# Attention with banded heads, then expert routing: masks by quadrants, a swapped half of v, routing steps and one weight load moved

## The chip, the cores and the metric

The kernel runs on one core of a Trainium2 chip. The metric is the device time of one execution in microseconds. Engines are named as in the profile: PE (matrix), DVE (vector), ACT (scalar), POOL (GpSimd) and SP (sync); PEld is the weight load of PE.

## The reference

```python
def _attn_ref(q, k, v, is_retrieval, n_sink, window):      # q, k, v: 4 x 8 x 768 x 64
    scores = scale * np.matmul(q, k.transpose(0, 1, 3, 2))
    rel = pos[:, None] - pos[None, :]
    causal = rel >= 0
    stream_keep = causal & ((pos[None, :] < n_sink) | ((rel >= 0) & (rel < window)))   # 4 and 64
    # heads with is_retrieval = [1,0,1,0,0,0,1,0] use causal, the others stream_keep
    a = softmax(where(mask, scores, -1e9))
    return np.matmul(a, v)

def _moe_ref(x, domain_id, w1, w2):                         # x: 3072 x 512, 8 experts
    for e in range(E):
        mask = domain_id == e
        out[mask] = np.maximum(x[mask] @ w1[e], 0.0) @ w2[e]   # w1: 512 x 1024, w2: 1024 x 512

x = attn_out.transpose(0, 2, 1, 3).reshape(B * S, H * D)
return _moe_ref(x, moe_domain_id, moe_w1, moe_w2)
```

Three of the eight heads attend to all earlier positions. The five others see a band of 64 positions and the first four positions ("sinks"). Every token then goes through the two layers of the one expert that its `domain_id` names.

## The kernel before

**Attention.** Heads are taken two at a time: `PAIRS = [(0, 2), (6, 7), (1, 3), (4, 5)]` for each of four batches, so 16 pairs, numbered n. The first pair of a batch has two full heads and six rounds, the second one full and one banded head and four rounds, the other two are fully banded with two rounds. Two rounds make a step, so these pairs have three, two, one and one steps. A pair goes through: load q, k (`load_qk`, L140) and v (`load_v`, L160) in float32 by SP's queue; cast to half precision on POOL (`cast_qk`, `cast_v`); twelve transposes on PE into qT and kT, copied out of PSUM by ACT or DVE (L303); masks and scores (`scores`, L306); exponentials on ACT (L341); the products with v (`av_items`, L345, with its matmuls at L384); division by the row sums on DVE (L396, L397). In qT and kT the first head of a pair has rows 0 to 63 and the second head rows 64 to 127.

Masks are added by the matrix engine before the scores: a matmul of the identity with a constant of 0 and -30000 (L313) writes the mask into PSUM, and the score matmuls (L330) add to it. In a banded head, keys are cut into blocks of 64. An even block's scores stand in partitions 0 to 63 and an odd block's in 64 to 127, each for 128 queries.

**Order of the work.** All queues run in the order in which the program writes them. The main loop (L846) takes pair n: `hooks(n)` puts out SP's loads for pair n + 4, POOL's casts for n + 2 and n + 1, the store of a finished batch's x (`store_x`, L409) and for some n the expert weights; then each step has the scores of pair n, followed by the transposes of pair n + 1 or the value products of pair n - 1. For the first pair the program writes the order out (L861). q and k have three float32 buffers each, v has four.

**Routing.** `routing_items` (L415) computes on DVE which token belongs in which slot of which expert. Its parts are put after given steps by a table from (pair, step) to functions (L632). They end with `map_i`, `map_e` (row numbers of x for gathers) and `out_i`.

**Experts.** `load_w(e, which)` (L191) loads one weight of 2 MB in float32 as 1 MB in half precision through POOL's queue. `load_xe(pr, g)` (L652) gathers 128 rows of x for slot group g of a pair of experts, also through POOL's queue. Groups 0, 1, 3, 4 of experts 0 to 3 gather from the first three batches (`map_e`), so they may start before the last batch is stored; the groups 2, 5 and 6 need all of x. PE transposes the rows (`x_transpose`, L665), multiplies with w1 (`layer1`, L694), ACT applies relu (L711), PE multiplies with w2 (L754, L768), DVE copies (L718), and POOL scatters the rows (L720). The order on PE is written out from L878: first 256 columns of experts 0 to 3, then the transposes of groups 2, 6 and 5 and the remaining columns, then the second layers.

Of the kernel before, what the change touches and what calls it, by code (L numbers as in the profile page):

```python
# [21 lines left out]
def kernel(  # L22
# [46 lines left out]
    up = jj >= 64  # L69
    cc = ii[:, :64]  # L70
    m_even = neg(np.where(up, cc < kk, cc >= kk))
    m_odd = neg(np.where(up, cc >= kk, cc < kk))
    m_first = neg((ii[:, :P] >= jj) & ((jj < NS) | (ii[:, :P] - jj < WIN)))
# [6 lines left out]
            m_first,  # L80
            np.tile(np.concatenate([m_even, m_odd], axis=1), (1, 4)),
# [7 lines left out]
    C_ID, C_DG, C_S0, C_S1, C_ST, C_ON, C_IO = (  # L89
        0, 128, 256, 384, 896, 1024, 1026)  # L90
# [68 lines left out]

    def load_v(b, pi):  # L160
        hA, hB = PAIRS[pi]
        t = vpool.tile([P, 2, NSO, D], FP32, tag="v32", name=f"v32_{b}_{pi}")
        for hh, h in enumerate((hA, hB)):
            nc.sync.dma_start(
                out=t[:, hh], in_=v[b, h].rearrange("(c p) d -> p c d", p=P)
            )
        v_t[b, pi] = t
# [57 lines left out]
    def s_bin(col, hh, part):  # L225
        res = []
        q0, q1 = ((0, 512), (512, S))[part]

        def add(k0, m, o, i0, w, kind="band"):
            lo, hi = max(i0, q0), min(i0 + w, q1)  # L230
            if lo < hi:
                res.append((col + lo - q0, hi - lo, hh, k0, m, o, lo, (hh, kind)))

        for o in (0, 64):
            add(o, 64, o, 0, P)
        for it in range(NSO):
            k0 = it * P
            if it:
                add(k0, 64, 0, k0, P)
            add(k0 + 64, 64, 64, k0 + (64 if it else P), P if it else 64)  # L240
        if part == 1:
            for r in range(4):
                i0 = (P, 3 * P, 4 * P, 4 * P)[r]
                res.append((col + 256, 256, hh, 0, 32, 32 * r, i0, (hh, "s", r)))
        return res

    def plan(ra, rb):

        dg = lambda c: (c, P, C_DG)
        s0 = lambda c: (c, 512, C_S0)  # L250
        s1 = lambda c: (c, 256, C_S1)
        if ra and rb:
            return [
                (r_bin(0 if n < 5 else 384, 0, n), r_bin(512, 1, n),
                 [dg(0 if n < 5 else 384), dg(512)], 0 if n < 5 else 384,
                 1024 if n < 5 else 640)
                for n in range(6)
            ]
        if ra:
            return [  # L260
                (r_bin(0, 0, 0, 64), s_bin(512, 1, 0), [dg(0), s0(512)], 0, 1024),
                (r_bin(0, 0, 1, 64), s_bin(512, 1, 1), [(0, P, C_DG), s1(512)], 0, 1024),
                (r_bin(0, 0, 2), r_bin(512, 0, 3), [dg(0), dg(512)], 0, 1024),
                (r_bin(384, 0, 5), r_bin(512, 0, 4), [dg(384), dg(512)], 384, 1024),
            ]
        return [
            (s_bin(0, 0, 0), s_bin(512, 1, 0), [s0(0), s0(512)], 0, 1024),
            (s_bin(0, 0, 1), s_bin(512, 1, 1), [s1(0), s1(512)], 0, 1024),
        ]
# [36 lines left out]
    def scores(n, rounds):  # L306
        sps = {}
        for r in rounds:
# [3 lines left out]
            for c, w, col in plans[n % 4][r][2]:  # L312
                nc.tensor.matmul(  # L313
                    out=sp[:, c : c + w],
                    lhsT=id_sb,
                    rhs=c16[:, col : col + w],
                    start=c // 512 not in begun,
                    stop=True,
                    skip_group_check=True,
                )  # L320
                begun.add(c // 512)
# [23 lines left out]
    def av_items(n):  # L345
# [5 lines left out]
        def make(hh, h):  # L351
# [8 lines left out]
            else:  # L360
                full.append((slice(0, P), band(0), ve[:, 0, h, :], 0, 0, P))
                for it in range(1, NSO):
# [4 lines left out]
                    )  # L367
                for it in range(1, NSO):
                    low.append((slice(0, 64), band(it * P), ve[0:64, it, h, :], it, 0, P))
                    for m0 in (64, 0):  # L370
                        jt = it if m0 else it - 1
                        upp.append(
                            (slice(64, P), band(it * P + m0), ve[64:P, jt, h, :], it, m0, 64)
                        )
# [32 lines left out]
        return (fa + fb, la + lb + ua + ub) if lb else (fa, fb)  # L407
# [7 lines left out]
    def routing_items():  # L415
# [194 lines left out]
        def rows3():  # L610
# [22 lines left out]
            (0, 0): (one_hot,), (0, 1): (ranks, scan, own, place, place2, split),  # L633
            (1, 0): (high,), (2, 0): (high2,), (3, 0): (high3,), (4, 1): lows[0:1],
            (4, 2): lows[1:2], (5, 1): (flags,), (6, 0): lows[2:3], (7, 0): lows[3:4],
            (8, 1): lows[4:5], (8, 2): lows[5:6], (10, 0): (rows,), (11, 0): (rows2,),
            (12, 1): (rows3,),
# [142 lines left out]
    nc.scalar.dma_start(out=c16[:, 0:C_S0], in_=c16_d[:, 0:C_S0])  # L780
    load_qk(0)
    load_v(0, 0)
    nc.sync.dma_start(out=dom64[:], in_=moe_domain_id.rearrange("(p c) -> p c", p=P))
    nc.sync.dma_start(out=c32[:], in_=c32_d)
    load_qk(1)
    nc.sync.dma_start(out=c16[:, C_S0:], in_=c16_d[:, C_S0:])
    load_v(0, 1)
# [15 lines left out]
    def hooks(n):  # L803
# [13 lines left out]
        if n == 6:  # L817
            load_w(0, 1)
        if n == 13:
# [26 lines left out]
    for n in range(NPAIR + 1):  # L846
# [13 lines left out]
        if n == 0:  # L860
            tr, av0, av1 = [lambda: keep_warm(3, 0)], [lambda: keep_warm(3, 1)], tr  # L861
# [7 lines left out]
    store_x(B - 1)  # L869
    for g in (2, 6, 5):  # L870
        load_xe(0, g)
    load_w(0, 2)
# [164 lines left out]
```

The softmax here doesn't subtract the row's maximum and nothing guards it: scores larger than these inputs give would overflow.

## Time and profile before

| what | value |
|---|---|
| time, median of 4 | 217.18 us (215.89 to 218.42) |
| profiled execution | 218.96 us, span 217.2 us |
| busy share PE, PEld | 87%, 57% |
| busy share DVE, ACT, POOL | 43%, 41%, 55% |
| mean granted PE clock | 0.931 |
| POOL's queue (q0) | 26.80 MB, 54.5% of 16 DMA engines |
| SP's queue (q1) | 22.50 MB, 37.7% |

The shares are means over a span of two unlike halves. A row of the page's slices is one fortieth of the span, 5.4 us, and a digit is tenths. In tables by stage each engine has its busy microseconds with the number of instructions, and then come the granted clock, the DMA share (over 1 where several transfers overlap) and GB/s. In a timeline a line is start, length, engine, source line and operation, and in brackets how long the engine was idle before it and what released it. The page's instruction queues, 19 packets with 0.31 MB and 10 with 0.08 MB, are the fetches of the program itself.

### The profile page before, as it was taken

The numbers are of one execution on the slowest core, as the hardware profiler recorded it, in microseconds if no ns is written. First come the engines' busy times: TensorE is split into PE (matmuls) and PEld (weight loads), VectorE is DVE, ScalarE is ACT, GpSimd is POOL, SyncE is SP. The second block draws the span as 40 slices with busy tenths as digits, with TensorE's granted clock in tenths as the row PEclk, the third lists the DMA queues.
The fourth block names the chain that finished last, engine by engine and source line by source line (L and its number), as shares of the span: only waits on it lengthen the run. The fifth ranks groups of instructions, "written<-read, shape, count | busy, mean of one in ns | idle before, by whom it ended". The sixth has DMA issues, their size and how long they took to land. (4 is left out here: it accounts for less than half of the span.)

```text
span 217.2 us, 5394 instructions
## 1 busy us (share of the span) xinstructions
PE 188.4 (87%) x2256; PEld 124.5 (57%) x2256; DVE 93.6 (43%) x200; ACT 89.9 (41%) x115; POOL 118.9 (55%) x154
## 2 busy tenths in 40 slices
PE   7653997999899898788997999999969999999930
PEld 2332774777578575447997885456534555444420
DVE  4566778478886984052112105520144300333320
ACT  2461687567877975302664560025500156000000
POOL 7737678395166457840287844627776510450571
PEclk9995898599999999659999999999999999999995
DMA  6999999999999988999359999999799999981232
GB/s 186 297 276 307 304 266 259 308 331 233 292 297 319 320 254 149 208 237 201 133 114 210 208 256 235 203 280 289 159 197 211 273 216 224 278 259 51 94 143 90
DMA packets 44447, 49.76 MB, mean 229 GB/s; under 512 B 28799, under 2 KB 37376, under 8 KB 44418
## 3 DMA queue, kind: packets, MB, share of 16 engines
q0 software_dynamic: 9472, 26.80, 54.5%
q1 hardware_dynamic: 34802, 22.50, 37.7%
q8 instruction: 19, 0.31, 0.6%
q10 hardware_dynamic: 144, 0.07, 0.2%
q14 instruction: 10, 0.08, 0.1%
HBM read 56.73 MB, written 10.49 MB: 310 GB/s over the span
## 5 line engine op out<-in xcount | busy, mean ns | idle before, releaser
L341 ACT ACTIVATE eT<-sp 128x1024 f16<-128x1024 f32 (+2 forms) x56 | 50.0, 953 | 23.5 <-PE sp L330 18.6
L711 ACT ACTIVATE hT<-h 128x512 f16<-128x512 f32 (+2 forms) x48 | 31.7, 668 | 61.4 <-PE h L704 58.6
L704 PE MATMUL h<-xT,w 128*128 128x256 f16 (+2 forms) x384 | 50.7, 290 | 2.3 <-DVE xT L683 1.1
L720 POOL DMA_INDIRECT out_dram<-oute,out_i x27 | 27.2, 1006 | 39.0 <-DVE oute L718 25.7
L704 PEld LDWEIGHTS <-w 128*128 128x128 f16 x384 | 39.0, 114 | 12.7 <-issue 1.6
L754 PE MATMUL o<-w,hT 128*128 128x512 f16 x184 | 41.9, 379 | 0.0
L718 DVE COPY oute<-o 128x512 f32<-128x512 f32 x23 | 15.9, 692 | 51.3 <-PE o L754 45.5
L754 PEld LDWEIGHTS <-hT 128*128 128x128 f16 x184 | 17.5, 98 | 19.8 <-issue 0.8
L384 PEld LDWEIGHTS <-eT 128*128 128x128 f16 (+2 forms) x672 | 22.5, 106 | 10.8 <-issue 8.2
L330 PE MATMUL sp<-qT,kT 64*64 64x128 f16 (+8 forms) x468 | 21.8, 258 | 7.1 <-DVE kT L303 6.3
L384 PE MATMUL av<-ve,eT 128*128 128x65 f16 (+2 forms) x572 | 23.5, 202 | 4.2 <-DVE kT L303 1.6
L155 POOL CAST q<-q 128x768 f16<-128x768 f32 x15 | 13.0, 865 | 24.8 <-DMA q<-in_q_dram 19.4
L654 POOL DMA_INDIRECT xe<-x_tok,map_i x16 | 16.3, 1020 | 16.3 <-SPq L941 11.8
L689 DVE COPY xT<-xtp 128x1024 f16<-128x1024 f16 (+1 forms) x16 | 8.9, 554 | 25.4 <-PE xtp L676 25.4
L330 PEld LDWEIGHTS <-kT 64*64 64x64 f16 (+2 forms) x468 | 10.6, 105 | 15.2 <-DVE kT L303 6.7
L397 DVE TENSOR_TENSOR xb<-av,rcp 128x384 f16<-128x384 f32 x32 | 17.8, 558 | 1.1
L313 PE MATMUL sp<-c16s 128*128 128x128 f16 (+2 forms) x112 | 16.9, 272 | 0.0
L175 POOL CAST ve<-v 128x384 f16<-128x384 f32 x32 | 16.4, 539 | 0.0
L155 POOL CAST k<-k 128x768 f16<-128x768 f32 x15 | 13.2, 880 | 4.8 <-DMA k<-in_k_dram 3.9
L396 DVE RECIPROCAL rcp<-av 128x6 f32<-128x6 f32 x32 | 6.1, 192 | 17.0 <-PE av L384 9.8
L313 PEld LDWEIGHTS <-c16s 128*128 128x128 f16 x112 | 8.7, 104 | 3.7 <-issue 1.2
L746 ACT COPY oute_last<-o_last 128x128 f32<-128x128 f32 x2 | 0.5, 266 | 24.7 <-DVE oute_last L746 23.2
(96 smaller groups left out, 177.3 us busy)
## 6 DMA issues: line engine op xcount, KB each, us to landing
w<-in_moe_w_dram POOLq DMA_DIRECT2D x16, 1024.0 KB
q<-in_q_dram SPq DMA_DIRECT2D x16, 384.0 KB, 6.2
k<-in_k_dram SPq DMA_DIRECT2D x16, 384.0 KB, 6.0
v<-in_v_dram SPq DMA_DIRECT2D x32, 192.0 KB, 6.1
x_tok<-xb SPq DMA_DIRECT2D x4, 768.0 KB, 6.3
out_dram<-oute,out_i POOLq DMA_INDIRECT x27
xe<-x_tok,map_i POOLq DMA_INDIRECT x16
c16s<-c SPq DMA_DIRECT2D x1, 224.5 KB, 6.3
```

The source lines that it names most:

```text
L155: eng.tensor_copy(out=t[:].rearrange("p t h d -> p h t d"), in_=q32_t[nm, n][:])
L175: nc.gpsimd.tensor_copy(out=ve_t[b][:, :, h, 0:D], in_=v_t[b, pi][:, hh])
L313: nc.tensor.matmul(out=sp[:, c : c + w], lhsT=id_sb, rhs=c16[:, col : col + w], start=c // 512 not in begun, stop=True, skip_group_check=True,
L330: nc.tensor.matmul(out=sp[o : o + m, c : c + w], lhsT=kT[n][rows, k0 : k0 + m], rhs=qT[n][rows, i0 : i0 + w], start=False, stop=True, skip ...
L341: nc.scalar.activation(out=eT[n, r // 3][:, r % 3, c0:c1], in_=sp[:, c0:c1], func=AF.Exp, scale=scale)
L384: nc.tensor.matmul(out=ps[m0 : m0 + m, it, :], lhsT=eT[n, r // 3][rows, r % 3, c : c + m], rhs=rhs, start=(cell["n"] == 1), stop=(cell["n" ...
L397: nc.vector.tensor_tensor(out=xb[b][:, :, h * D : (h + 1) * D], in0=ps[:, :, 0:D], in1=rcp[:].unsqueeze(2).to_broadcast([P, NSO, D]), op=A ...
L654: nc.gpsimd.indirect_dma_start(out=xe_of(pr, g), out_offset=None, in_=x_d[0 : 1 + nb * S, :], in_offset=bass.IndirectOffsetOnAxis(ap=(map_ ...
L704: nc.tensor.matmul(out=pv[:, a, c0:c1], lhsT=w_t[e, 1][:, c // 2, c % 2, fc * 512 + fr : (fc + 1) * 512 : 4], rhs=xT_t[e][:, c, c0:c1], st ...
L711: nc.scalar.activation(out=hT_t[e][:, 2 * f2 : 2 * f2 + 2, c0:c1], in_=pv[:, :, c0:c1], func=AF.Relu)
L720: inst = nc.gpsimd.indirect_dma_start(out=out, out_offset=bass.IndirectOffsetOnAxis(ap=out_i[:, s : s + 1], axis=0), in_=o[:], in_offset=None,
L754: nc.tensor.matmul(out=ps[:], lhsT=hT_t[e][:, f, g * P : (g + 1) * P], rhs=w_t[e, 2][:, f // 4, f % 4, :], start=(f == 0), stop=(f == 7),)
```

## The change

- *Masks.* A banded head's mask is no longer one matmul of 128x128 with the identity, but two of 64x64, each with a 64x64 corner of the identity and its own half of the constant. The constants of the two heads stand in their own rows, so `C_S0`, `C_S1` become `C_SE`, `C_SO`. The constant grows from 1154 to 1538 columns.
- *Swapped halves.* In a pair of two banded heads the second head's even blocks go to partitions 64 to 127 and its odd blocks to 0 to 63. Its v is loaded with halves exchanged to match, by two DMAs of 64 partitions for one of 128. The value matmuls of the two heads then alternate.
- *Routing.* Its parts start one pair later and are spread over more steps; `flags` comes last.
- *Start.* q, k, v of pair 1 and the rest of the mask constant are loaded before `dom64` and `c32`; pair 1 is transposed after the second step of pair 0, no longer after its third.
- *Weights.* w1 of expert 0 is loaded at pair 13 together with that of expert 1, instead of at pair 6. w2 of expert 0 is issued before the first gathers that need all of x, instead of after three of them.

```diff
     BIG = 30000.0
     neg = lambda keep: np.where(keep, 0.0, -BIG)
     kk = jj % 64
-    up = jj >= 64
     cc = ii[:, :64]
-    m_even = neg(np.where(up, cc < kk, cc >= kk))
-    m_odd = neg(np.where(up, cc >= kk, cc < kk))
-    m_first = neg((ii[:, :P] >= jj) & ((jj < NS) | (ii[:, :P] - jj < WIN)))
+    below, above = neg(cc >= kk), neg(cc < kk)
+    first = lambda j: neg((ii[:, :P] >= j) & ((j < NS) | (ii[:, :P] - j < WIN)))
     m_diag = neg(jj <= ii[:, :P])
     strict = (jj < np.arange(P)[None, :]).astype(np.float64)
     c16_np = np.concatenate(
         [
             np.eye(P),
             m_diag,
-            m_first,
-            np.tile(np.concatenate([m_even, m_odd], axis=1), (1, 4)),
+            first(kk),
+            np.tile(np.concatenate([below, above], axis=1), (1, 3)),
+            first(kk + 64),
+            np.tile(np.concatenate([above, below], axis=1), (1, 3)),
             strict,
             np.ones((P, 1)),
             jj < 3 * 32,
...
         ],
         axis=1,
     ).astype(np.float16)
-    C_ID, C_DG, C_S0, C_S1, C_ST, C_ON, C_IO = (
-        0, 128, 256, 384, 896, 1024, 1026)
+    C_ID, C_DG, C_SE, C_SO, C_ST, C_ON, C_IO = (
+        0, 128, 256, 768, 1280, 1408, 1410)
     NHI = NSLOT // P
     step = np.ones((E, NT))
     step[:, 0] = 0.0
...
             )
             qk_t[nm, n] = t
 
+    def swapped(pi, hh):
+        return hh == 1 and not any(retr[h] for h in PAIRS[pi])
+
     def load_v(b, pi):
         hA, hB = PAIRS[pi]
         t = vpool.tile([P, 2, NSO, D], FP32, tag="v32", name=f"v32_{b}_{pi}")
         for hh, h in enumerate((hA, hB)):
-            nc.sync.dma_start(
-                out=t[:, hh], in_=v[b, h].rearrange("(c p) d -> p c d", p=P)
-            )
+            if swapped(pi, hh):
+                src = v[b, h].rearrange("(c x p) d -> x p c d", x=2, p=64)
+                nc.sync.dma_start(out=t[64:P, hh], in_=src[0])
+                nc.sync.dma_start(out=t[0:64, hh], in_=src[1])
+            else:
+                nc.sync.dma_start(
+                    out=t[:, hh], in_=v[b, h].rearrange("(c p) d -> p c d", p=P)
+                )
         v_t[b, pi] = t
 
     def cast_v(b, pi):
...
             c += w
         return res
 
-    def s_bin(col, hh, part):
+    def s_bin(col, hh, part, swap=0):
         res = []
         q0, q1 = ((0, 512), (512, S))[part]
 
         def add(k0, m, o, i0, w, kind="band"):
             lo, hi = max(i0, q0), min(i0 + w, q1)
             if lo < hi:
-                res.append((col + lo - q0, hi - lo, hh, k0, m, o, lo, (hh, kind)))
+                res.append((col + lo - q0, hi - lo, hh, k0, m, o ^ swap, lo, (hh, kind)))
 
         for o in (0, 64):
             add(o, 64, o, 0, P)
...
 
     def plan(ra, rb):
 
-        dg = lambda c: (c, P, C_DG)
-        s0 = lambda c: (c, 512, C_S0)
-        s1 = lambda c: (c, 256, C_S1)
+        dg = lambda c: [(c, P, slice(0, P), slice(0, P), C_DG)]
+
+        def sm(hh, part, swap=0):
+            rows = slice(64 * hh, 64 * hh + 64)
+            w, d = ((512, 0), (256, P))[part]
+            return [
+                (512 * hh, w, rows, slice(o ^ swap, (o ^ swap) + 64), c + d)
+                for o, c in ((0, C_SE), (64, C_SO))
+            ]
+
+        mix = lambda a, b: [x for ab in zip(a, b) for x in ab]
         if ra and rb:
             return [
                 (r_bin(0 if n < 5 else 384, 0, n), r_bin(512, 1, n),
-                 [dg(0 if n < 5 else 384), dg(512)], 0 if n < 5 else 384,
+                 dg(0 if n < 5 else 384) + dg(512), 0 if n < 5 else 384,
                  1024 if n < 5 else 640)
                 for n in range(6)
             ]
         if ra:
             return [
-                (r_bin(0, 0, 0, 64), s_bin(512, 1, 0), [dg(0), s0(512)], 0, 1024),
-                (r_bin(0, 0, 1, 64), s_bin(512, 1, 1), [(0, P, C_DG), s1(512)], 0, 1024),
-                (r_bin(0, 0, 2), r_bin(512, 0, 3), [dg(0), dg(512)], 0, 1024),
-                (r_bin(384, 0, 5), r_bin(512, 0, 4), [dg(384), dg(512)], 384, 1024),
+                (r_bin(0, 0, 0, 64), s_bin(512, 1, 0), dg(0) + sm(1, 0), 0, 1024),
+                (r_bin(0, 0, 1, 64), s_bin(512, 1, 1), dg(0) + sm(1, 1), 0, 1024),
+                (r_bin(0, 0, 2), r_bin(512, 0, 3), dg(0) + dg(512), 0, 1024),
+                (r_bin(384, 0, 5), r_bin(512, 0, 4), dg(384) + dg(512), 384, 1024),
             ]
         return [
-            (s_bin(0, 0, 0), s_bin(512, 1, 0), [s0(0), s0(512)], 0, 1024),
-            (s_bin(0, 0, 1), s_bin(512, 1, 1), [s1(0), s1(512)], 0, 1024),
+            (s_bin(0, 0, p), s_bin(512, 1, p, 64), mix(sm(0, p), sm(1, p, 64)), 0, 1024)
+            for p in range(2)
         ]
 
     plans = [plan(retr[a], retr[c]) for a, c in PAIRS]
...
             sp = ps_s.tile([P, 1024], FP32, tag="sp", name=f"sp_{n}_{r}")
             sps[r] = sp
             begun = set()
-            for c, w, col in plans[n % 4][r][2]:
+            for c, w, rows, o, col in plans[n % 4][r][2]:
                 nc.tensor.matmul(
-                    out=sp[:, c : c + w],
-                    lhsT=id_sb,
-                    rhs=c16[:, col : col + w],
-                    start=c // 512 not in begun,
+                    out=sp[o, c : c + w],
+                    lhsT=c16[rows, C_ID + rows.start : C_ID + rows.stop],
+                    rhs=c16[rows, col : col + w],
+                    start=(c // 512, o.start) not in begun,
                     stop=True,
                     skip_group_check=True,
                 )
-                begun.add(c // 512)
+                begun.add((c // 512, o.start))
         for r in rounds:
             la, lb, _, c0, c1 = plans[n % 4][r]
             sp = sps[r]
...
                         (slice(0, P), col_of(tiles, (hh, "s", r), it * P),
                          vs_t[r, b // 2][:, b % 2 * H + h - 1, :], it, 0, P)
                     )
+                ra, rb = (slice(0, 64), slice(64, P))[:: -1 if swapped(pi, hh) else 1]
                 for it in range(1, NSO):
-                    low.append((slice(0, 64), band(it * P), ve[0:64, it, h, :], it, 0, P))
+                    low.append((ra, band(it * P), ve[ra, it, h, :], it, 0, P))
                     for m0 in (64, 0):
                         jt = it if m0 else it - 1
-                        upp.append(
-                            (slice(64, P), band(it * P + m0), ve[64:P, jt, h, :], it, m0, 64)
-                        )
+                        upp.append((rb, band(it * P + m0), ve[rb, jt, h, :], it, m0, 64))
             total = len(full) + len(low) + len(upp)
 
             def mm(item):
...
             return [[lambda x=x: mm(x) for x in l] for l in (full, low, upp)]
 
         (fa, la, ua), (fb, lb, ub) = [make(hh, h) for hh, h in enumerate(PAIRS[pi])]
-        return (fa + fb, la + lb + ua + ub) if lb else (fa, fb)
+        if la:
+            mix = lambda a, b: [x for ab in zip(a, b) for x in ab]
+            return fa + fb, mix(la, lb) + mix(ua, ub)
+        return (fa + fb, lb + ub) if lb else (fa, fb)
 
     def store_x(b):
         nc.sync.dma_start(
...
 
         lows = [lambda t=t: low(t) for t in range(0, NT, 4)]
         return {
-            (0, 0): (one_hot,), (0, 1): (ranks, scan, own, place, place2, split),
-            (1, 0): (high,), (2, 0): (high2,), (3, 0): (high3,), (4, 1): lows[0:1],
-            (4, 2): lows[1:2], (5, 1): (flags,), (6, 0): lows[2:3], (7, 0): lows[3:4],
-            (8, 1): lows[4:5], (8, 2): lows[5:6], (10, 0): (rows,), (11, 0): (rows2,),
-            (12, 1): (rows3,),
+            (1, 0): (one_hot,), (1, 1): (ranks,), (2, 0): (scan,), (3, 0): (own,),
+            (4, 0): (place,), (4, 1): (place2,), (4, 2): (split,), (5, 0): (high,),
+            (6, 0): (high2,), (7, 0): (high3,), (8, 0): lows[0:1], (8, 1): lows[1:2],
+            (8, 2): lows[2:3], (9, 0): lows[3:4], (9, 1): lows[4:5], (10, 0): lows[5:6],
+            (11, 0): (rows,), (12, 0): (rows2,), (12, 1): (rows3,), (12, 2): (flags,),
         }
 
     xe_t, xT_t, hT_t = {}, {}, {}
...
 
 
     nc.vector.memset(zrow[:], 0.0)
-    nc.scalar.dma_start(out=c16[:, 0:C_S0], in_=c16_d[:, 0:C_S0])
+    nc.scalar.dma_start(out=c16[:, 0:C_SE], in_=c16_d[:, 0:C_SE])
     load_qk(0)
     load_v(0, 0)
+    load_qk(1)
+    nc.sync.dma_start(out=c16[:, C_SE:], in_=c16_d[:, C_SE:])
+    load_v(0, 1)
     nc.sync.dma_start(out=dom64[:], in_=moe_domain_id.rearrange("(p c) -> p c", p=P))
     nc.sync.dma_start(out=c32[:], in_=c32_d)
-    load_qk(1)
-    nc.sync.dma_start(out=c16[:, C_S0:], in_=c16_d[:, C_S0:])
-    load_v(0, 1)
     load_qk(2)
     load_v(0, 2)
     nc.scalar.preload_act_table(AF.Exp)
...
             cast_v((n + 1) // 4, (n + 1) % 4)
         if n >= 5 and n % 4 == 1:
             store_x(n // 4 - 1)
-        if n == 6:
+        if n == 13:
             load_w(0, 1)
-        if n == 13:
             load_w(1, 1)
         if n == 14:
             for g in (0, 1, 3, 4):
...
         if R == 1:
             run(tr)
         if n == 0:
-            tr, av0, av1 = [lambda: keep_warm(3, 0)], [lambda: keep_warm(3, 1)], tr
+            tr, av0, av1 = [lambda: keep_warm(3, 0)], tr, [lambda: keep_warm(3, 1)]
         steps = {1: [av0 + av1], 2: [tr, av0 + av1], 3: [tr, av0, av1]}[R]
         for x, step in enumerate(steps):
             if n < NPAIR:
...
             for fn in route.get((n, x), ()):
                 fn()
     store_x(B - 1)
+    load_w(0, 2)
     for g in (2, 6, 5):
         load_xe(0, g)
-    load_w(0, 2)
     for g in (2, 6, 5):
         load_xe(1, g)
     load_w(1, 2)
```

## The prediction

> **What bounds the kernel now.** I read the page's slices first, then the busy time by stage, then the timeline of each engine around the stage borders, then the chain. The slices show two halves. Up to about 98 us it is attention, from there to 211 us the expert layers.
>
> ```profile
> PE   7653997999899898788997999999969999999930
> PEclk9995898599999999659999999999999999999995
> DMA  6999999999999988999359999999799999981232
> ```
>
> The DMA row is 9 from 5 to 80 us. PE has holes there, and its clock falls twice to 5 tenths near 18 and 40 us. In the second half PE is full to 206 us. The table by stage tells what the DMA row hides:
>
> ```profile
> 8.00:45.00 37.00, 28.81 (x471) 19.77 (x472) 25.83 (x54) 21.78 (x25) 23.42 (x38) 0.82 1.15 291
> 45.00:57.00 12.00, 11.02 (x265) 8.38 (x262) 9.98 (x24) 9.80 (x12) 6.81 (x11) 1.00 1.07 275
> 57.00:79.00 22.00, 21.16 (x475) 15.63 (x472) 17.36 (x44) 17.64 (x21) 11.38 (x18) 1.00 1.10 304
> 80.00:106.00 26.00, 22.34 (x328) 16.46 (x325) 8.09 (x19) 8.85 (x13) 12.52 (x16) 0.80 0.89 203
> 174.00:184.00 10.00, 10.00 (x55) 5.84 (x53) 0.00 (x0) 6.18 (x7) 0.76 (x1) 1.00 1.06 216
> ```
>
> The last two columns are the DMA share and GB/s. Until 79 us the queues carry about 300 GB/s without a pause, whatever PE does, so attention runs at the pace of q, k and v. The timeline confirms it at the last pair, where the cast of k waits for its DMA and the transposes follow 0.4 us after that cast:
>
> ```profile
> 20.02 1.40 PE L330 MATMUL sp<-qT,kT 64*64 64x512 f16 x24 [5.47 <-DVE kT L303]
> ...
> 79.34 0.83 POOL L155 CAST k<-k 128x768 f16<-128x768 f32 x1 [0.25 <-DMA k<-in_k_dram]
> 80.60 0.50 PE L294 MATMUL tp<-c16s,q 128*128 128x128 f16 x6
> 81.02 0.72 POOL L194 DMA_DIRECT2D w<-in_moe_w_dram  x1
> 89.21 1.94 ACT L341 ACTIVATE eT<-sp 128x1024 f16<-128x1024 f32 x2 [4.74 <-remote]
> 92.36 0.20 DVE L396 RECIPROCAL rcp<-av 128x6 f32<-128x6 f32 x1 [5.36 <-remote]
> 107.15 1.00 POOL L654 DMA_INDIRECT xe<-x_tok,map_i  x1 [11.78 <-SPq L941]
> 110.77 0.77 POOL L201 DMA_DIRECT2D w<-in_moe_w_dram  x1
> 115.00 0.39 PE L676 MATMUL xtp<-c16s,xe 128*128 128x128 f16 x4
> ```
>
> Read three facts here. The 5.47 us hole at 14.5 us is DVE working off the routing before it copies kT. From 85 to 92 us PE, ACT and DVE wait for nothing of the program ("issue" and "remote"). The first gather over all batches is issued only when the last x store has landed: that store was issued at 97.24 and is the one with the longest landing, 9.1 us, thus 106.3. During that wait DMA runs dry (0.49 of 104 to 106, nothing of 106 to 108). From 115.00 PE runs almost without holes to 208.7, apart from the wait at the end of this piece of the chain:
>
> ```profile
> 153.25 0.53 POOL w L194
> 153.78 0.23 issue
> 154.01 0.02 POOLq L654
> 154.03 0.32 issue
> 154.35 8.80 DMA xe<-x_tok,map_i
> 163.15 0.05 issue
> 163.19 0.40 PE xtp L676 x4
> ```
>
> A gather that moves 131 KB landed after 8.8 us, because a weight was issued just ahead of it.
>
> [...]So a gather on POOL's queue stands behind the weights issued before it; the 8.8 us above agrees. [...]the 36 score matmuls of a banded pair (5120 columns) pass in 0.71 us (26.67 to 27.38). [...]here 5.47 us cost the clock, 2.0 us at 161 us did not. [...]
>
> **The change part by part.** The sum is made against the profiled execution: span 217.2, own time 218.96 us. That is 1.8 above the median of 217.18, so I move the median by the difference.
>
> *Masks.* In a fully banded pair four matmuls of 512, 512, 256 and 256 columns by the whole array (25.93 to 26.67, 0.74 us) become eight of 64x64, four at a time in different quadrants: 768 columns instead of 1536, about 0.4 us saved in each of 8 pairs, 3.2 us of PE. Bounds: zero, if the quadrants do not overlap, and 0.45. In the mixed pair both quadrants lie in the same rows, so nothing is saved[...]. *Swapped v.* The 30 half-height value matmuls of a banded pair take 0.84 us (31.44 to 32.28), 28 ns each; the scores go at 20 ns when the rows alternate, so I take 0.24 us for each of 8 pairs, bounds 0 and 0.4. SP issues 8 more DMAs of at least 0.4 us, while it mostly waits for room anyway (q issues have a median of 1.4 us). The head whose v is swapped ends together with its partner, which delays the first rcp by some 0.3 us; nobody is late by that.
>
> *Routing spread and pair 1 transposed earlier.* DVE's work of 12.5 to 18.2 us no longer stands before qT and kT. k_1 can be cast by 11 us (its load is issued 1.9 us sooner, ahead of dom and c32), so scores of pair 1 start near 14 instead of 20.02. What is late next: q_2 and k_2, whose cast ended at 17.2 before. PE gains 4 us there and then runs into the supply. The same holds for masks and v: the supply covers them. If it did not, PE alone could have been at pair 15 by about 69 us, 6 to 7 us earlier than I put it below.
>
> *First weight from round 6 to 13.* From 45 to 57 us the queues moved 3.30 MB, of which 1.05 MB is that weight. At 304 GB/s 3.65 MB would have passed: 1.40 MB of q, k, v were displaced, 4.6 us. Its own time from the stage at 174 us, where weights pass alone: 1.05 MB / 216 GB/s = 4.85 us, so the two agree. The mask constants grow by 384 columns, 98 KB, 0.3 us. Net 4.3 us: the cast of k_15 ends at 75.9 instead of 80.17, the first weight issue moves from 81.02 to 76.7.
>
> *What POOL's ring holds then.* Before the first gather over all batches it now carries five weights, not three: w1 of experts 0 to 3 and w2 of expert 0, which was hoisted ahead of the gathers. A gather: 80 to 106 us holds 26 x 0.89 = 23.1 us of DMA, less 14.6 for three weights, 2.6 for the last x store (0.79 MB at 300 GB/s) and about 1 for the rest of v and the x store before; eight gathers share 4.9, 0.61 each. Ring start 76.7 + 1.0 = 77.7; 5 x 4.85 = 24.3; 9 x 0.61 = 5.5; x store 2.6; rest of the x store before 1.0; landing after the last packet 1.3 (105 to 106.3 above). Sum: the gather for (0, 2) lands at 112.4.
>
> *PE at that point.* The gathers of expert 0 land at 77.7 + 9.7 + 2.4 + 1.3 = 91.1, so PE could start them near 91.5 (98.3 before) and be at L676 for (0, 2) 16.7 us later, at 108.2, perhaps 109.5 after a wait for w1 of expert 3. It then waits 3 to 4 us for the gather. Before, PE came at 115.00 and the gather was there. So of 4.3 us of supply and of the 5 us of dry DMA that the hoisted w2 fills, 115.0 - 112.4 = 2.6 us are left. After it nothing is nearer: w2 of expert 0 has landed, the other weights stand some 5 us earlier against PE than before, and the 2 us wait at 161 us stays, since POOL issues those gathers behind PE's own progress.
>
> **Forecast and rivals.**
>
> A (0.48): the ring sets it, as worked out: 217.18 - 2.6 = 214.6. Each of the five weights at 4.6 or 5.2 us and an issue 1 us sooner or later give 212.4 to 217.4.
>
> B (0.20): the saving passes through. If transfers overlap more than the 216 GB/s of single weights suggests, PE is not held at (0, 2): 115.0 - 108.2 = 6.8, time 210.4. For it speaks that 168 to 170 us moved 363 GB/s; against it that outputs were in that mix.
>
> C (0.16): the wait at (0, 2) lasts long enough to halve the clock[...]. For it: 5.47 us of idleness did so at 14.5 us.[...]
>
> D (0.16), slower: the crawl of 85 to 92 us grows. It began 4 us after one weight was issued on POOL's ring with gathers behind it. Now two weights come together while pairs 14 and 15 are still to run. The way from pair 15's transposes to the expert layers was 17.7 us (80.6 to 98.3); the work in it is about 9.3 (pair 14 its 3.57 less 0.6; pair 15 masks 0.35, scores 0.71, values 1.3; then warming 0.9 and 1.5 at full clock, values 1.3), so the crawl cost 8.4. If it doubles, expert work starts at 76.3 + 9.3 + 16.8 = 102.4 and the end moves by +4.1 to 221.3. It decides from a crawl of about 12.7 us on (98.3 - 85.6). Against it: PE is further along in the program when the ring fills.
>
> That quadrants do not overlap is a rival to the masks' 0.4 us, but changes the end in none of A to D, since supply covers it.
>
> **How the numbers follow.** About 1% is what a measurement of this kernel can tell from no change, 2.2 us. The border is 215.0: of A's 212.4 to 217.4 a little over half lies below it, its middle too, so of its 0.48 0.30 is faster and 0.18 within; with B 0.20 and a short loss of clock 0.02 faster is 0.52. C gives else 0.12 within[...]; D gives 0.16 slower. That is faster 0.52, same 0.30, slower 0.18. The range reaches to B's 210.4 and, above, halfway into D: 210.2 to 219.2. A's own range is 212.4 to 217.4. The time is A's.
>
> **What would show it.** In the profile after: no hole before the scores of pair 1, L313 in banded pairs at about 0.35 us; k_15 cast by 76 us; DMA above 0.9 from 80 to 110 without the dry stretch at 106; PE idle for some us before L676 at about 110 with the gather's DMA as the releaser. The forecast is wrong if the last cast of k is not earlier (then supply was not what held it), if PE does not wait for that gather (B), or if the remote waits at the end of attention are longer than 8 us (D).

## The result and the profile after

The change made the kernel slightly slower, where 1.2% faster had been forecast: 218.26 us median against 217.06 us, ratio 1.0062 with a 95% interval of 1.004 to 1.0084, so +1.35 us. A ratio compares only executions that were not in the chip's slower state, while a median is of all. The profiled execution of after (217.0 us, span 215.1) lies below its median and that of before (218.96) above its own, so spans are not compared here, only when things happen in them.

The DMA row of the page's slices, after:

```profile
DMA  6999999999999998999999999998899999961232
```

The dry stretch that the DMA row showed near 106 us is gone, as forecast. What one must not conclude from a row of nines is that the same work is passing: it is a share of time, not of bytes. The table by stage (busy time of each engine with instructions, granted clock, DMA share, GB/s) has the bytes:

```profile
8.00:45.00 37.00, 31.11 (x521) 21.35 (x521) 24.81 (x54) 22.79 (x26) 21.77 (x35) 0.82 1.18 273
45.00:57.00 12.00, 10.49 (x271) 7.58 (x270) 9.96 (x18) 9.94 (x12) 7.84 (x12) 1.00 1.14 299
57.00:79.00 22.00, 20.37 (x482) 15.40 (x482) 20.92 (x52) 17.61 (x22) 11.83 (x19) 1.00 1.15 276
80.00:106.00 26.00, 20.27 (x323) 15.72 (x321) 7.45 (x17) 9.27 (x13) 15.60 (x19) 0.93 1.00 225
```

In the stages of 8 to 45 and 57 to 79 us the queues moved 273 and 276 GB/s, where before moved 291 and 304, although the DMA share is higher (1.18 and 1.15 against 1.15 and 1.10). The stage between them (299 against 275) can't be compared so: before's had the weight among its bytes. More time per byte: that is the signature of transfers that became less efficient. The page's row of SP's queue points the same way. The first line is after's; 37.7% were needed before for 22.50 MB:

```profile
q1 hardware_dynamic: 34930, 22.60, 41.8%
...
v<-in_v_dram SPq DMA_DIRECT2D x24, 192.0 KB, 6.4
...
v<-in_v_dram SPq DMA_DIRECT2D x16, 96.0 KB, 6.7
```

The 0.10 MB added are the longer mask constant. The 16 transfers of 96 KB are the eight swapped loads in two halves each, and a half takes as long to land as a whole one (6.7 against 6.4 us). Neither number is proof by itself: `after_noswap` below loads v whole and still has 39.6%, and in `chunks_in_before`, where 96 KB fill all partitions, they land in 5.7 us and 192 KB in 5.8. The timeline of after, at the places that the prediction named:

```profile
15.82 0.86 PE L346 MATMUL sp<-qT,kT 64*64 64x512 f16 x24
22.39 0.52 PE L329 MATMUL sp<-c16s 64*64 64x512 f16 x8
22.74 0.75 PE L346 MATMUL sp<-qT,kT 64*64 64x128 f16 x36
28.63 0.61 PE L399 MATMUL av<-ve,eT 64*128 64x65 f16 x30
...
78.86 0.83 POOL L155 CAST k<-k 128x768 f16<-128x768 f32 x1 [0.71 <-DMA k<-in_k_dram]
...
94.56 0.76 PE L694 MATMUL xtp<-c16s,xe 128*128 128x128 f16 x8 [0.62 <-DMA xe<-x_tok,map_e]
...
114.66 0.40 PE L694 MATMUL xtp<-c16s,xe 128*128 128x128 f16 x4
```

Everything on PE came as priced: the 5.47 us hole before the scores of pair 1 is gone, the masks of a banded pair take 0.35 us from start to the scores' start (0.74 before), its 30 value matmuls are shorter (0.61 us, 0.91 before). But the last cast of k, which should have begun near 75, begins at 78.86; before it was 79.34. A weight of 1.05 MB had left the stretch in which q, k and v are loaded, and the loads were hardly earlier. That is the whole question.

### The profile page after: what moved, and what is told of

The parts are those of the page before. It is cut to its first block, busy times and chain, and to the rows that moved or that the text cites. A ratio compares the mean times of both kernels' runs of the same rounds, so it can differ in the third digit from the quotient of the medians.

```text
span 215.1 us, 5489 instructions
## 1 busy us (share of the span) xinstructions
PE 185.2 (86%) x2296; PEld 121.9 (57%) x2296; DVE 95.0 (44%) x200; ACT 89.6 (42%) x115; POOL 119.2 (55%) x154
## 3 DMA queue, kind: packets, MB, share of 16 engines
q1 hardware_dynamic: 34930, 22.60, 41.8%
## 4 chain that ended last, share of the span: by engine, by line
PE 52%; DMA 21%; DVE 7%; POOL 6%; issue 5%; SPq 5%; POOLq 1%; ACT 1%
PE h L722 19%; PE o L772 19%; DMA k<-in_k_dram 12%; DMA xe<-x_tok,map_e 6%; PE o2h L786 3%; DMA q<-in_q_dram 3%; PE sp L346 2%; PE av L399 2%; PE xtp L694 2%; POOL xe L672 2%; SPq L145 2%; POOL out_dram L738 1%; DVE kT L319 1%; POOL k L155 1%; SPq L170 1%
## 5 line engine op out<-in xcount | busy, mean ns | idle before, releaser
L399 PEld LDWEIGHTS <-eT 128*128 128x128 f16 (+2 forms) x672 | 20.2, 104 | 10.9 <-issue 8.5
L399 PE MATMUL av<-ve,eT 128*128 128x65 f16 (+2 forms) x572 | 22.0, 201 | 4.0 <-issue 2.3
L346 PE MATMUL sp<-qT,kT 64*64 64x128 f16 (+8 forms) x468 | 21.3, 250 | 0.6 <-DVE kT L319 0.6
L329 PE MATMUL sp<-c16s 128*128 128x128 f16 (+2 forms) x152 | 16.1, 290 | 1.9 <-issue 0.9
L183 POOL CAST ve<-v 128x384 f16<-128x384 f32 x32 | 17.4, 572 | 0.0
L155 POOL CAST k<-k 128x768 f16<-128x768 f32 x15 | 12.6, 839 | 7.1 <-DMA k<-in_k_dram 5.7
L346 PEld LDWEIGHTS <-kT 64*64 64x64 f16 (+2 forms) x468 | 11.3, 103 | 7.6 <-issue 2.8
L694 PE MATMUL xtp<-c16s,xe 128*128 128x128 f16 x96 | 8.4, 220 | 3.2 <-DMA xe<-x_tok,map_e 3.1
L319 DVE COPY qT<-tpq 128x768 f16<-128x768 f16 x8 | 7.6, 952 | 7.8 <-PE tpq L310 7.7
L764 ACT COPY oute_last<-o_last 128x128 f32<-128x128 f32 x2 | 0.5, 266 | 24.7 <-DVE oute_last L764 23.2
```

The lines of the kernel that those rows point to most:

```text
L155: eng.tensor_copy(out=t[:].rearrange("p t h d -> p h t d"), in_=q32_t[nm, n][:])
L183: nc.gpsimd.tensor_copy(out=ve_t[b][:, :, h, 0:D], in_=v_t[b, pi][:, hh])
L329: nc.tensor.matmul(out=sp[o, c : c + w], lhsT=c16[rows, C_ID + rows.start : C_ID + rows.stop], rhs=c16[rows, col : col + w], start=(c // 5 ...
L346: nc.tensor.matmul(out=sp[o : o + m, c : c + w], lhsT=kT[n][rows, k0 : k0 + m], rhs=qT[n][rows, i0 : i0 + w], start=False, stop=True, skip ...
L399: nc.tensor.matmul(out=ps[m0 : m0 + m, it, :], lhsT=eT[n, r // 3][rows, r % 3, c : c + m], rhs=rhs, start=(cell["n"] == 1), stop=(cell["n" ...
```

## The experiments

All ratios are to the kernel before on the same chip, with 95% intervals. Beside the time, each experiment is read by one line: the start of the last cast of k, which says when the supply of attention ends. That line is from one profiled execution of each kernel, and these can lie some microseconds above their kernel's median (that of `chunks_in_before` 222.22 us against 213.65), and the kernels ran on different chips (the median of before ranges from 212.78 to 218.73 us over them) while before was profiled once. So differences of a microsecond or two in it are not read.

**Do the halves alone, and take them alone away.** `halves_in_before` cuts eight loads of the kernel before into partition halves, without exchanging them:

```diff
+            if pi >= 2 and hh == 1:
+                src = v[b, h].rearrange("(c x p) d -> x p c d", x=2, p=64)
+                nc.sync.dma_start(out=t[64:P, hh], in_=src[1])
+                nc.sync.dma_start(out=t[0:64, hh], in_=src[0])
```

> The kernel before, with one thing added: in the 8 banded pairs the second head's v is loaded by two DMAs of 64 partitions, not exchanged. Theory H (half loads cost DMA time; SP's queue q1 took 41.8% of 16 engines' span after the change, 37.7% before, for the same bytes): q1 near 41%, the last cast of k on POOL 2 to 4 us later than 79.3 us, time 1 to 2% above before. Theory W (the order of the weights is what costs): q1 as before, time within 0.5% of before.

`after_noswap` is after with v loaded whole and no exchange; masks by quadrants, routing and weights stay:

```diff
     def swapped(pi, hh):
-        return hh == 1 and not any(retr[h] for h in PAIRS[pi])
+        return False
...
-            (s_bin(0, 0, p), s_bin(512, 1, p, 64), mix(sm(0, p), sm(1, p, 64)), 0, 1024)
+            (s_bin(0, 0, p), s_bin(512, 1, p), mix(sm(0, p), sm(1, p)), 0, 1024)
```

> The kernel after, with v of the banded pairs loaded whole and no halves exchanged; quadrant masks, routing, start and weights as after. Theory H: q1 back to about 38%, the last cast of k near 75 us (78.9 after), time 1 to 2% below after, so 0.5 to 1.5% below before. Theory W: time as after, 0.3 to 1% above before.

Measured: `halves_in_before` 1.0213 (1.0157 to 1.027), `after_noswap` 0.9877 (0.9818 to 0.9937). The last cast of k, in the timelines of halves_in_before and then of after_noswap:

```profile
83.61 0.83 POOL L155 CAST k<-k 128x768 f16<-128x768 f32 x1 [0.61 <-PE av L389]
```

```profile
74.15 0.83 POOL L155 CAST k<-k 128x768 f16<-128x768 f32 x1 [0.31 <-DMA k<-in_k_dram]
```

Both ways about the same size: cutting eight loads moves it 4.3 us later (79.34 to 83.61), making them whole moves it 4.7 us earlier (78.86 to 74.15). The stage 8 to 45 us follows, halves_in_before and then after_noswap:

```profile
8.00:45.00 37.00, 29.43 (x485) 20.17 (x486) 25.39 (x55) 22.07 (x26) 22.08 (x35) 0.86 1.18 269
```

```profile
8.00:45.00 37.00, 31.93 (x663) 22.28 (x663) 26.77 (x60) 26.09 (x30) 23.53 (x38) 0.95 1.17 292
```

269 and 292 GB/s, against 291 before and 273 after. So the loads in halves turn the forecast's gain into the measured loss; `after_noswap` also gives up the exchange, which `after_castswap` below keeps. What makes them slow was still open: that there are eight more DMAs, that each is of 96 KB, or that each fills only half of the partitions.

**More of them, as many by another cut, and other halves.** Three kernels on the base of before. `chunks_in_before` cuts the same eight loads by key blocks, so that each part is 96 KB and fills all 128 partitions:

```diff
+                nc.sync.dma_start(out=t[:, hh, 0:3], in_=src[:, 0:3])
+                nc.sync.dma_start(out=t[:, hh, 3:6], in_=src[:, 3:6])
```

> The kernel before, with the same loads cut in two as in halves_in_before, but by blocks of 128 keys (two DMAs of 96 KB over all 128 partitions). Theory P (what costs is that a load fills only 64 partitions): q1 near 38%, time within 0.5% of before. Theory N (what costs is the number and size of the DMAs): q1 near 41%, time 1.5 to 2.5% above before, as in halves_in_before.

`halves_twice` cuts the loads of both heads of each banded pair into partition halves, 16 loads instead of 8:

```diff
-            if pi >= 2 and hh == 1:
+            if pi >= 2:
```

> The kernel before, with v of both heads of the banded pairs loaded by halves of 64 partitions (16 loads cut, not 8). If half loads cost supply time, the cost doubles: q1 near 45%, last cast of k about 8 us later than 79.3, time 3.5 to 5% above before. If the loss in halves_in_before was an accident of where the loads fall, it doesn't double: 2 to 3%.

`every_second` cuts eight loads into two of 64 partitions again, but takes the even and the odd ones:

```diff
+                src = v[b, h].rearrange("(c p y) d -> y p c d", y=2, p=64)
+                nc.sync.dma_start(out=t[0:P:2, hh], in_=src[0])
+                nc.sync.dma_start(out=t[1:P:2, hh], in_=src[1])
```

> The kernel before, with v of the second head of each banded pair again loaded by two DMAs of 64 partitions each, but of every second partition (0, 2, ... 126, then 1, 3, ... 127) instead of 0 to 63 and 64 to 127; the layout stays as before. Sixteen DMAs of 96 KB, as in halves_in_before and chunks_in_before. Theory P (which partitions[...]): like chunks_in_before, last cast of k begins at 78.5 to 80 us, ratio 0.998 to 1.009. Theory N (how many partitions: [...]that alone makes it slow): like halves_in_before, last cast of k begins at 83 to 84.5 us, ratio 1.015 to 1.027.

The last cast of k in chunks_in_before, halves_twice and every_second, in this order:

```profile
78.87 0.83 POOL L155 CAST k<-k 128x768 f16<-128x768 f32 x1 [0.34 <-DMA k<-in_k_dram]
```

```profile
87.32 0.83 POOL L155 CAST k<-k 128x768 f16<-128x768 f32 x1 [0.61 <-DMA k<-in_k_dram]
```

```profile
77.57 0.83 POOL L155 CAST k<-k 128x768 f16<-128x768 f32 x1 [0.34 <-DMA k<-in_k_dram]
```

| loads cut, and how | DMAs added | last cast of k, us | ratio |
|---|---|---|---|
| none (before) | 0 | 79.34 | 1 |
| 8, by blocks, 128 partitions each | 8 | 78.87 | 1.004 (0.9992 to 1.0088) |
| 8, even and odd partitions, 64 each | 8 | 77.57 | 1.0012 (0.9968 to 1.0055) |
| 8, partitions 0 to 63 and 64 to 127 | 8 | 83.61 | 1.0213 (1.0157 to 1.027) |
| 16, partitions 0 to 63 and 64 to 127 | 16 | 87.32 | 1.0479 (1.0424 to 1.0535) |

Eight more issues on SP cost nothing that can be seen (1.004 by blocks, 1.0012 by even and odd partitions); the cover that the prediction named for them holds. The size of 96 KB costs nothing clear of the noise either (1.004, from 0.9992). Nor does the number of partitions: 64 are as good as 128 when they are every second one (1.0012, 0.9968 to 1.0055). The lower or the upper half is what costs, about 0.5 us of supply for each load so cut (4.3 us / 8, and 8.0 / 16; 0.75 if `every_second` at 77.57 is the base). SP's share of queue time missed what was expected of it three times: 41.8% in `halves_twice`, not 45, hardly more than 41.4% with eight cut, and 39.6 and 39.9% in `after_noswap` and `after_castswap`, not 38. The share is of packets' times, and does not grow in step with the delay; the start of the cast does. Why a part that stays in partitions 0 to 63 or 64 to 127 is slower, no run here shows; they give its price.

**The exchange elsewhere.** `after_castswap` loads v whole and exchanges the halves when POOL casts:

```diff
+            if swapped(pi, hh):
+                for o in (0, 64):
+                    nc.gpsimd.tensor_copy(
+                        out=ve_t[b][64 - o : P - o, :, h, 0:D], in_=v_t[b, pi][o : o + 64, hh]
+                    )
```

> The kernel after, with the halves exchanged on POOL, in the cast of v (two casts of 64 partitions for one of 128), so that v is loaded whole. Theory H: as without exchange, q1 about 38%, time 0.5 to 1.5% below before; POOL has some 0.5 us more per banded pair. Theory W: time as after, 0.3 to 1% above before.

Measured 0.9923 (0.9866 to 0.998), last cast of k at 74.48. After itself, with the same exchange made by half loads, has 1.0062 and 78.86. So the exchange as such is no harm; its place in the DMA was. It also keeps what the exchange was worth on PE. The 30 value matmuls of a banded pair, in after_castswap and then in after_noswap:

```profile
36.02 0.60 PE L400 MATMUL av<-ve,eT 64*128 64x65 f16 x30
```

```profile
27.77 0.92 PE L399 MATMUL av<-ve,eT 64*128 64x65 f16 x30
```

The 0.3 us saved in each of eight pairs do not show in the time, though: the intervals of the two kernels overlap, and `after_noswap` has the lower mean. POOL pays for it, busy 123.8 us against 118.7.

**What is left of the sum: PE's part and the weights' part.** The change moves two weights, w1 and w2 of expert 0, though its title counts one. `after_old_weights` is after, and `noswap_old_weights` is after_noswap, with both weights where before has them; `new_weights_only` is before with nothing but the two weight moves. The edit of the first two (the third is its inverse, on before):

```diff
-        if n == 13:
+        if n == 6:
             load_w(0, 1)
+        if n == 13:
             load_w(1, 1)
...
-    load_w(0, 2)
     for g in (2, 6, 5):
         load_xe(0, g)
+    load_w(0, 2)
```

> The kernel after, with the first expert's two weights where they were before: w1 at pair 6, w2 behind the first three gathers. Theory H: supply is worse still (half loads and w1 together), the last cast of k near 83 us, time 1 to 2% above before. Theory W: time below after by 0.5 to 1.5%, at or below before.

> The kernel after, without exchanged halves and with both weights where they were before: what is left is quadrant masks, value matmuls in turn, routing and start. Theory S (supply of q, k, v sets attention's end, so what PE and DVE save is covered): last cast of k at 79 us, time within 0.5% of before. Rival E (the early stall and the masks are worth their time): 1% or more below before.

> The kernel before with the two weight moves alone (w1 of expert 0 to pair 13, w2 of expert 0 ahead of the gathers over all batches). Theory S (supply and POOL's ring set the time, savings on PE and DVE are covered): last cast of k at 74 to 75 us, time 1 to 1.5% below before, as after_noswap. Rival E (the weights pay only with a faster PE): within 0.5% of before.

| | v whole, ratio | last cast of k | half loads, ratio | last cast of k |
|---|---|---|---|---|
| before's PE and routing, old weights | 1 | 79.34 | 1.0213 (1.0157 to 1.027) | 83.61 |
| before's PE and routing, new weights | 0.9965 (0.9912 to 1.0017) | 73.15 | not run | |
| after's PE and routing, old weights | 1.0049 (1.0009 to 1.009) | 77.54 | 1.0259 (1.0177 to 1.0341) | 84.92 |
| after's PE and routing, new weights | 0.9877 (0.9818 to 0.9937) | 74.15 | 1.0062 (1.004 to 1.0084) | 78.86 |

`after_old_weights` is a little worse than expected (84.92 for about 83, 2.6% for 1 to 2%). With the weights where they were, all that was gained on PE and DVE brings nothing, as "the supply covers them" said. With the weights moved but PE as before, supply ends 6.2 us sooner and the time moves by no more than its uncertainty: `new_weights_only` came out as the rival that its expectation names. Its timeline suggests why. The transposes of pair 15 and the first gather in new_weights_only:

```profile
79.83 0.50 PE L294 MATMUL tp<-c16s,q 128*128 128x128 f16 x6
...
88.36 1.10 POOL L654 DMA_INDIRECT xe<-x_tok,map_e  x1 [11.09 <-DVE xb L397]
```

The last k is cast at 73.15, but PE reaches pair 15's transposes only at 79.83, nearly as late as before (80.60), and the first gather, which reads rows that attention must have written, waits 11.09 us. In `after_noswap` these transposes stand at 76.43 and that gather at 79.55. Yet in `noswap_w2_behind` (below), whose program is the same up to that gather and whose ratio is no worse, it stands at 90.69, in an execution of 219.65 us (its median is 216.28):

```profile
90.69 1.10 POOL L672 DMA_INDIRECT xe<-x_tok,map_e  x1 [12.79 <-DVE rcp L411]
```

So single executions don't settle when that gather comes. What the ratios show is that the two parts gain 1.2% together, where the weights alone gain 0.35% and the rest alone loses 0.5%; the intervals of `new_weights_only` and `after_noswap` still touch. That PE's work in attention is the bound once supply is freed is argued, not shown. Which of PE's and DVE's savings lets the gain pass was not tested; the value products are not among them, since without the exchange they take 0.92 us, as before (0.91).

**One weight each, and one step further.** Three variants of after_noswap. `noswap_w2_behind` moves w2 of expert 0 back behind the first three gathers over all batches; `noswap_w1_at_6` leaves w2 where the change put it and loads w1 of expert 0 at pair 6 again; `noswap_w11_later` moves w1 of experts 1, 2 and 3 each one place later, so that only one weight stands ahead of the first gathers:

```diff
         if n == 13:
             load_w(0, 1)
-            load_w(1, 1)
         if n == 14:
             for g in (0, 1, 3, 4):
                 load_xe(0, g, 3)
+            load_w(1, 1)
...
```

> The kernel after without exchanged halves and with w2 of expert 0 behind the first three gathers again; w1 stays at pair 13. The prediction's term: the gather for (0, 2) stands behind w2 of expert 0, 4.85 us; if PE waits on it, this runs 1 to 2% faster than after_noswap, 0.97 to 0.98 of before. In after_noswap PE came to (0, 2) at 110.13 without a wait, so the rival expects no gain: 0.985 to 0.995, the dry stretch of DMA during the x store being what w2 fills.

> The kernel after without exchanged halves and with w1 of expert 0 at pair 6 again; w2 of expert 0 stays ahead of the gathers. Supply theory: last cast of k at 78 to 79 us, 4 us later than in after_noswap, but one weight less on POOL's ring before the first gathers, so PE waits for them less: between after_noswap and noswap_old_weights, 0.99 to 1.005 of before. If the gain of after_noswap lies in w2 alone, this is 0.985 to 0.99.

> The kernel after without exchanged halves, and with w1 of expert 1, 2 and 3 each one place later on POOL's queue: w1 of expert 0, four gathers, w1 of 1, two gathers, w1 of 2, two gathers, w1 of 3. In after_noswap PE waits 3.48 us for the first gathers, at 90.4 us, behind both weights. If POOL's ring sets that wait, one weight less ahead (4.85 us) removes it and the time falls by 1 to 1.5% below after_noswap, to 0.97 or 0.975 of before. If later weights then hold PE instead, the time is that of after_noswap, 0.985 to 0.99.

| w1 of expert 0 | w2 of expert 0 | ratio |
|---|---|---|
| at pair 6 | behind three gathers | 1.0049 (1.0009 to 1.009) |
| at pair 6 | ahead of them | 1.0234 (1.0176 to 1.0292) |
| at pair 13 | behind three gathers | 0.9833 (0.9795 to 0.987) |
| at pair 13 | ahead of them | 0.9877 (0.9818 to 0.9937) |

The gain comes with w1's move. Hoisting w2 doesn't help: with w1 at pair 6 it costs 1.8% (1.0234 / 1.0049, from two chips), where 0.99 to 1.005 had been expected; with w1 at 13 the intervals overlap. `noswap_w2_behind` has the lowest ratio of this study, and lies between its two expectations (0.97 to 0.98, and 0.985 to 0.995). Why the hoist costs so much with w1 at pair 6 stays open. The first gather over all batches waits 11.39 us there and is issued at 109.78, but in before it waits as long (11.78). What stands out in the trace is the stall that rival D spoke of: DVE waits 7.5 us "remote" at the end of attention, and the granted clock is 0.50 from 90 to 106 us (an execution of 224.95 us, median 222.96). In the slices of `noswap_w1_at_6` these are the three fives:

```profile
PEclk9999999999769999555997999999999999999995
```

`noswap_old_weights` has no such wait, and its clock is 1.00 there. Whether the hoist brings the stall was not tested.

The third variant lost 2.7% against its base: 1.014 (1.0059 to 1.0221) where 0.97 to 0.975 was expected, or 0.985 to 0.99 by the rival. From its timeline:

```profile
86.94 1.12 POOL L672 DMA_INDIRECT xe<-x_tok,map_e  x1 [8.94 <-DMA x_tok<-xb]
92.02 0.79 POOL L202 DMA_DIRECT2D w<-in_moe_w_dram  x1
...
104.11 3.52 PE L722 MATMUL h<-xT,w 128*128 128x256 f16 x16 [5.98 <-DMA w<-in_moe_w_dram]
```

The gather waits 8.94 us for a store of x. The weight that now stands behind it in POOL's program is issued at 92.02 (about 76.6 in `after_noswap`), and PE stands 5.98 us for it. So the weight that `after_noswap` has ahead of the gathers is not only a burden on the ring; it was issued 15.4 us sooner there.

## Why the prediction was wrong, point by point

- **Swapped v: the step that failed.** "SP issues 8 more DMAs of at least 0.4 us, while it mostly waits for room anyway" was true of the issues (`chunks_in_before` 1.004, `every_second` 1.0012) and priced the wrong thing. The transfers were taken to be as efficient in halves; the term was zero and measured 4.3 to 4.7 us of supply. The delay can be followed from `after_noswap` to after: the last cast of k is 4.7 us later, the first weight issue too (75.83 to 80.54), the first expert transposes 4.1 (90.43 to 94.56), those of (0, 2) 4.5 (110.13 to 114.66). The ratio of the two is 1.0062 / 0.9877 = 1.0187, 4.1 us of 217; against `after_castswap`, which keeps the exchange, it is 1.014, 3.0 us. With the first of these -2.6 + 4.1 = +1.5, and +1.35 was measured; that is no second proof, as `after_noswap` had itself measured -2.6. The direction of the forecast hung on this one term, and none of the rivals contained it. Of the signs of being wrong, "the last cast of k is not earlier" came, but not what it was to mean: supply was what held it, and the half loads had used up what the weight had freed. On PE the exchange was worth 0.3 us a pair, 0.24 in the forecast.
- **First weight from round 6 to 13.** Right. Without half loads the last cast of k ends at 74.15 + 0.83 = 75.0 (forecast 75.9) and the first weight is issued at 75.83 (76.7). `new_weights_only` shows 6.2 us of supply for the two weight moves, where 4.6 had been worked out, a difference that single executions can't settle (the longer mask constant, which made them 4.3 net, is not in this kernel).
- **A's total.** For the kernel without half loads -2.6 us had been the forecast, and -1.23% of 212.8 us is -2.6. The sum agrees partly by luck, as the next point shows.
- **What POOL's ring holds then, and PE at that point.** The forecast had PE wait at the first gathers until about 91.1, and then 3 to 4 us for the gather (0, 2), which was to land at 112.4. In after_noswap:

```profile
90.43 1.20 PE L694 MATMUL xtp<-c16s,xe 128*128 128x128 f16 x8 [3.48 <-DMA xe<-x_tok,map_e]
...
110.13 0.39 PE L694 MATMUL xtp<-c16s,xe 128*128 128x128 f16 x4
```

  The first wait is there, 3.48 us and within 0.7 us of the forecast. The second is not: the line of 110.13, PE's arrival at (0, 2), has no bracket. The ring's sum was too long by at least 2.2 us, and PE's way from the first gathers to there was 19.7 us instead of 16.7. Most of these 3 us went with the clock, which was 0.50 from 90 to 96 us (0.87 in the mean of 80 to 106): the first 16 products with w1 took 3.57 us, 1.91 before. In after itself PE waits 0.62 us at 94.56 and not at 114.66, but it waits at the gathers between:

```profile
103.17 0.68 PE L694 MATMUL xtp<-c16s,xe 128*128 128x128 f16 x8 [1.23 <-DMA xe<-x_tok,map_e]
108.64 0.74 PE L694 MATMUL xtp<-c16s,xe 128*128 128x128 f16 x8 [1.29 <-DMA xe<-x_tok,map_e]
```

  So the gathers did hold PE, only not the one of (0, 2). After starts its expert layers 3.7 us sooner than before (94.56 against 98.30) and is 0.3 us ahead at (0, 2) (114.66 against 115.00).
- **Masks.** Right in size: 0.39 us a pair (0.74 to 0.35). In the mixed pair nothing is saved, as forecast: from the masks' start to the scores' start 0.65 us in before (58.38 to 59.03) and in after (15.17 to 15.82). "The supply covers them" holds while the weights are where they were (1.0049), and seems not to when they are moved (0.9877 with after's PE, 0.9965 with before's); the masks were not tested alone.
- **Routing spread and pair 1 transposed earlier.** Right in kind: the hole is gone. The scores of pair 1 start at 15.82 in after and at 14.86 in after_noswap, where 14 was forecast.
- **D, the slower rival.** The time rose, but not for its reason: from pair 15's transposes to the first expert transposes after takes 15.5 us (79.10 to 94.56), before 17.7, so the crawl did not grow. The work listed there adds up to 9.0 us, not 9.3, which changes nothing. Remote waits at that place are seen in before (5.4 us on DVE, 4.7 on ACT), in after (4.9) and in `noswap_w1_at_6`, and in none of the other eleven profiles; what brings them is open. **C** needed a long wait at (0, 2), and there was none; the clock of 80 to 106 us is 0.93 in after, above before's 0.80. A loss of clock like C's came in `after_noswap`, at the first gathers: 0.50 from 90 us, where a wait of 3.48 us ended. When the clock falls, and for how long, is not settled by the 5.47 us hole: in before it stood at 0.50 from 16.36 to 23.2 us, from 1.8 us into that hole, and again from 36.84 to 43.68, where PE had just had holes of 0.86 and 0.52 us. So how much time C would lose, and the 0.02 of slower beyond D's 0.16, were the author's estimate, which no trace bears out.
- **"The 2 us wait at 161 us stays."** Not in this execution. The chain of after at that place:

```profile
161.13 0.45 PE xtp L694 x8
```

  PE goes on to these transposes without a gather in the chain. That gain is part of what after_noswap has; its share was not measured apart. The wait is not in the profiles of `halves_in_before` and `chunks_in_before` either, which have before's order there.

## What to carry to other kernels

When a load is cut, look at which partitions each part fills: parts of 0 to 63 and 64 to 127 cost 0.5 us of supply each load of 192 KB here, the same cut by key blocks or by every second partition nothing that shows, and an exchange of halves can be made in a copy that is there anyway. Where a stage runs at the pace of its queues, as 8 to 45 us does here, price an edit to a load in bytes per second (291 GB/s before, 273 after), not in issues (eight more cost nothing that shows): compare GB/s and the DMA share together, since a share that rises (1.15 to 1.18) while GB/s falls is work that became less efficient. And where two limits lie close together, price what each edit is worth after the other, not only alone.

## What the runs showed of the hardware that was not expected

- Two DMAs of 64 partitions cost 4.3 us over eight loads when each stays in one half of the partitions, and nothing that shows (77.57 against 79.34, ratio 1.0012) when each takes every second one.
- A DMA of half the size took as long to land in full queues: 6.7 us for 96 KB and 6.4 us for 192 KB in after, and also 5.7 and 5.8 us in `chunks_in_before`, where both fill all partitions.
- In `noswap_w11_later` a gather on POOL's queue waited 8.94 us for a store; the weight behind it was issued only at 92.02 us (about 76.6 in `after_noswap`), and PE waited 5.98 us for it.
